# Pooled attention followed by a bilinear MoE: the planner's cost table is set to other values

## The chip, the cores and the metric

The kernel runs on one core of a Trainium2 chip. The metric is the device time in microseconds (us) of one execution; a figure is the median of several timed runs. A profile is one further execution, taken by the hardware profiler. Engines: PE is TensorE, with PEld its weight loads; DVE is VectorE, ACT is ScalarE, POOL is GpSimd, and SP is SyncE, which here only issues DMAs.

## The reference

Attention over 4 batches, 8 heads, 1152 positions and head width 64, with queries averaged in pairs (576 per head), feeds a bilinear layer of 1536 hidden columns; all in float32:

```python
q_pool = q.reshape(B, H, S // 2, 2, D).mean(axis=3)
scores = (1 / sqrt(D)) * q_pool @ k.transpose(0, 1, 3, 2)
attn = softmax(scores)                     # with + 1e-9 below the fraction
x = (attn @ v) as (4 * 576, 512)           # tokens x model width
out = ((x @ w_a) * (x @ w_b)) @ w_out      # 512 -> 1536 -> 512
```

## The kernel before

**Work.** A head pair p (16 of them, four per batch) is one step of attention. Its 576 queries and two heads are nine softmax blocks of 128 rows by 1152 keys, 144 in all. For a block, TensorE makes the scores (`qk`, `qk_rest`, L535 in float32 for batch 0 and L538 in f16 pieces for the other batches) into a PSUM tile `sps` that holds two blocks. VectorE scales them into SBUF with the row's minimum of the negated score (`sm_max`, L566), ScalarE takes the exponential with its row sum (`sm_exp`, L573), VectorE makes the reciprocal (`sm_sum`, `sm_rec`, L577 and L583), ScalarE writes the f16 high part of the probability (`sm_hi`, L586) and VectorE the low part (`sm_lo`, L590). SP then issues a transposing DMA of both parts (`transpose`, L596). When the blocks of a span of 256 or 320 queries are transposed, TensorE multiplies them with V (`pv`, 19 products, L622 and L632) into the one PSUM tile `xps`, ScalarE copies half of it out (`x_copy`, L641) and VectorE adds the other half (`x_add`, L647). ScalarE and GpSimd split x into f16 parts, and VectorE rescales them (`x_scale`, L684).

**MoE.** Nine token tiles of 256 tokens: two per batch (even and odd), and tile 8 with the 64 left over of each batch. A tile needs x of all four pairs of its batch. It is 24 steps of 12 products (`moe_mm`, L722), each pair of them gated by ScalarE and VectorE (`moe_a` L729, `moe_g` L734), and then 12 output steps of 6 products (`moe_o`, L748) on parts that ScalarE and GpSimd make (L739, L742). The f16 or rounded parts of the weights are made once, in the time of the first passes (`prep_w`, L423 to L495).

**Order.** Nothing of this order is written by hand. Every step is a task of a planner: `add(engine, duration, key, function, ..., r=, w=)` records what it reads and writes. `Plan.order` simulates five in-order engines, always giving an engine the ready task with the lowest key. It uses the durations, the table `LAT` for the delay from the end of a task on one engine (row) to the start of one that needs it on another (column), and for SP's tasks `DMA_START`, the issue time `gen`, one shared DMA channel that a transfer holds for its duration, `DMA_END` and a task's own `lag`. A task with `port=True` on VectorE keeps GpSimd's port tasks away while it runs. From each forward run the keys are made anew by a run backward in time; 20 trials with noise on the keys follow, 3 sweeps each, and the order of the shortest simulated run is emitted. Each engine then executes its own tasks strictly in that order, and waits where an input is late. The lines in question:

```python
start, length = self.run(key, False)
if best is None or length < best[0]:
    best = (length, key, start)
```

Of the kernel before, what the change touches and what calls it, by code (L numbers as in the profile page):

```python
# [19 lines left out]
NQ = S // 2  # L20
# [167 lines left out]
def kernel(  # L188
# [143 lines left out]
    def prep_qk(ps_, key):  # L332
        n = ps_.q1 - ps_.q0
        if ps_.split:
            u = f"ksc{ps_.u}"
            add("SP", 2.5, key - 3, load_k, (ps_.p, 0), w=["kn0"])
            add("SP", 2.5 * n / NQ, key - 3, load_q, (ps_.p, ps_.q0, ps_.q1), w=["qraw"])
            add("POOL", 0.1 + 1.55 * n / NQ, key, q_sum, (0, n), r=["qraw"], w=["qs0"])
            add("DVE", 1.35, key, k_max, (), r=["kn0"], w=["kmx0"])
            add("DVE", 0.1 + 0.6 * n / NQ, key, q_max, (n,), r=["qs0"], w=["kmx1"])  # L340
            add("PE", 0.45, key - 2, k_sum, (), r=["kmx0", "kmx1", "ones"], w=["xps"])
            add("DVE", 0.7, key - 2, k_scale, (ps_.u,), r=["xps"], w=[u])
            return
        if not ps_.again:
            add("SP", 2.5, key - 3, load_k, (ps_.p, ps_.jk), w=[f"kn{ps_.jk}"])
        add("SP", 2.5 * n / NQ, key - 3, load_q, (ps_.p, ps_.q0, ps_.q1), w=["qraw"])
        add("POOL", 0.1 + 1.55 * n / NQ, key, q_sum, (ps_.jq, n), r=["qraw"], w=[f"qs{ps_.jq}"])

    def split_qk(ps_, key):
        n = ps_.q1 - ps_.q0  # L350
        if ps_.split:
            u = f"ksc{ps_.u}"
            add("ACT", 1.25, key, k_hi, (ps_.u,), r=["kn0", u], w=["kn1"])
            add("ACT", 0.1 + 0.55 * n / NQ, key, q_hi, (ps_.u, n), r=["qs0", u], w=["qs1"])
            add("DVE", 1.45, key, k_lo, (ps_.u,), r=["kn0", u, "kn1"], w=["kn1l"], port=True)
            add("DVE", 0.1 + 0.65 * n / NQ, key, q_lo, (ps_.u, n), r=["qs0", u, "qs1"], w=["qs1l"], port=True)
# [43 lines left out]
    def prep_vmax(p, new, key):  # L400
        add("SP", 2.5, key - 3, load_v, (p,), w=["vraw"])
        if new:
            add("DVE", 1.3, key, v_max, (p,), r=["vraw"], w=[f"vmx{p}"])
            add("PE", 0.45, key - 2, v_sum, (p,), r=[f"vmx{p}", "ones"], w=["xps"])
            add("DVE", 0.5, key - 2, v_scale, (p,), r=["xps"], w=[f"vsc{p}"])
            if p % NP == NP - 1:
                b = p // NP
                add("DVE", 0.5, key, v_batch, (b,), r=[f"vsc{NP * b + j}" for j in range(NP)], w=[f"vb{b}"])

    def prep_v(p, key):  # L410
        add("ACT", 1.25, key, v_hi, (p,), r=["vraw", f"vsc{p}"], w=["vsh"])
        add("DVE", 1.4, key, v_lo, (p,), r=["vraw", "vsh", f"vsc{p}"], w=["vsl"], port=True)
# [85 lines left out]
    def prep_w(f, key):  # L498
        for m in range(3):
            n = 3 * f + m  # L500
            z, rw = f"z{zi(n)}", f"raw{n % NRAW}"
            add("SP", 2.2, key - 4, w_load, (f, m, n), w=[rw])
            add("ACT", 0.66, key, w_abs, (n,), r=[rw], w=[z])
            if m < 2:
                add("DVE", 0.74, key, w_max, (f, m, n), w=[z, f"wmx{f}{m}"])
            add("ACT", 0.66, key, w_tail, (n,), w=[rw + "l"], r=[rw])
            add("POOL", 2.45, key, w_sign, (n,), w=[rw + "l"], r=[rw], port=False)
            add("DVE", 0.68, key, w_join, (n,), r=[rw, rw + "l"], w=[z], port=True)
            if m == 1:
                add("DVE", 0.2, key, w_mag, (f,), r=[f"wmx{f}0", f"wmx{f}1"], w=[f"wal{f}"])  # L510
                add("PE", 0.45, key - 5, w_sum, (f,), r=[f"wal{f}", "ones"], w=["xps"])
                add("DVE", 0.2, key - 5, w_scale, (f,), r=["xps"], w=[f"wsd{f}"])
                add("DVE", 0.17, key, w_inv, (f,), r=[f"wsd{f}"], w=[f"wsc{f}"])
        for m in range(3):
# [4 lines left out]
            add("ACT", 0.7 if m < 2 else 0.66, key, w_hi, (f, m, n), r=[z] + ws, w=[f"w{f}{m}h"] + last)  # L519
            if m < 2:  # L520
                add("DVE", 0.73, key, w_lo, (f, m, n), r=[z, f"w{f}{m}h"] + ws, w=[f"w{f}{m}l"] + last, port=True)
            else:
                add("POOL", 1.6, key, w_lo, (f, m, n), r=[z, f"w{f}{m}h"], w=[f"w{f}{m}l"])
# [127 lines left out]
    def unit(ps_, e, c0, runs, key):  # L651
# [4 lines left out]
        add("PE", 0.155 + 2.16 * w / 384, key - 9, pv, (e, c0, w),  # L656
# [29 lines left out]
    def x_scales(b, which, key):  # L686
        for c in range(NP):
            for m in which:
                t = {"even": 0, "odd": 1, "rest": 2}[m]
                x = f"x{b % 2}{c}{t}" if t < 2 else f"xr{b}{c}"  # L690
                add("DVE", 0.35 if t < 2 else 0.15, key, x_scale, (NP * b + c, t), r=[f"vb{b}"], w=[x + "h", x + "l"], port=True)

    def x_split(ps_, which, key):
# [8 lines left out]
        add("ACT", 0.1 * len(which) + 0.6 * n, key, x_hi, (p, j, which), r=xs, w=[x + "h" for x in names] + alias)  # L702
        add("POOL", 0.1 * len(which) + 1.4 * n, key, x_lo, (p, j, which), r=xs + [x + "h" for x in names],
# [66 lines left out]
    def moe_ab(t, f0=0, f1=NF):  # L770
        bs = [t // 2] if t < 8 else list(range(B))
        xs = [f"x{t // 2 % 2}{c}{t % 2}{hl}" if t < 8 else f"xr{b}{c}{hl}" for b in bs for c in range(KC) for hl in "hl"]
        for f in range(f0, f1):
# [7 lines left out]
            for m in range(2):  # L781
                add("PE", 1.308, key + m, moe_mm, (t, f, m, j), r=r, w=[f"acc{j}"])
            add("ACT", 0.42 if t < 8 else 1.1, -1000, moe_a, (t, f, j), r=[f"acc{j}"] + scs, w=[f"g{f}"] + ([f"raw{1 + f // 4}"] if t == 0 and f >= 4 else []))
            add("DVE", 0.42 if t < 8 else 1.0, -1000, moe_g, (t, f, j), r=[f"acc{j}"] + scs, w=[f"g{f}"])

    def moe_last(t):
        key = 1000 + 3 * len(steps)
        for f in range(NF):
            j = len(outs) % NG
            outs.append((t, f))  # L790
            add("ACT", 0.41, key - 20, moe_gh, (f, j), r=[f"g{f}"], w=[f"gh{j}"])
            add("POOL", 0.72, key - 20, moe_gl, (f, j), r=[f"g{f}", f"gh{j}"], w=[f"gl{j}"])
            add("PE", 1.39, key - 1, moe_o, (f, j, f == 0, f == NF - 1),
# [159 lines left out]
```

## Time and profile before

| what | value |
|---|---|
| timed runs, median of 3 | 935.23 us (935.16 to 935.75) |
| profiled execution, its own time | 939.15 us |
| its span, first to last instruction | 937.4 us |
| PE, DVE, ACT, POOL busy | 792.7, 710.0, 600.6, 265.0 us |
| mean granted TensorE clock | 0.922 of full speed |

Busy time is the union of an engine's records; idle time has a releaser, the instruction or DMA that ended the wait. In-order queues mean that an instruction which waits holds up all behind it on its engine, whether they could run or not.

### The profile page before, as it was taken

How to read it: one execution, taken by the hardware profiler on the slowest of the kernel's cores; microseconds unless marked ns; L12 is line 12 of the kernel's file. 1: busy time of each engine (PE TensorE's matmuls, PEld its weight loads, DVE VectorE, ACT ScalarE, POOL GpSimd, SP SyncE). 2: the span in 40 equal slices, each digit the busy share in tenths (PEclk: the TensorE clock that was granted, in tenths of full speed). 3: DMA queues.
4: the chain of work that ended last, by engine and by line, in shares of the span. 5: the costliest groups of instructions: out<-in, count | busy, mean ns of one | idle time of the engine just before them, and what ended most of it. 6: DMA issues, size and time to landing. Idle time of an engine off the chain costs nothing.

```text
span 937.4 us, 15587 instructions
## 1 busy us (share of the span) xinstructions
PE 792.7 (85%) x5856; PEld 562.4 (60%) x5856; DVE 710.0 (76%) x1352; ACT 600.6 (64%) x973; POOL 265.0 (28%) x228
## 2 busy tenths in 40 slices
PE   4546436998789988669999999899999998999997
PEld 2323224665456755337766776576677666877885
DVE  6699999996799889998999799989889873112010
ACT  5677977966577768857787687667867762232212
POOL 4547687622311012111023113201310231110303
PEclk9666667999789999969999999999999999999999
DMA  7999799886989889987878979979786674000100
GB/s 254 235 205 243 201 236 221 222 188 121 198 174 157 155 164 195 206 167 146 174 156 167 176 152 161 199 130 175 150 162 141 103 151 76 1 23 2 23 1 23
DMA packets 353644, 141.40 MB, mean 151 GB/s; under 512 B 338208, under 2 KB 340256, under 8 KB 353568
## 3 DMA queue, kind: packets, MB, share of 16 engines
q1 hardware_dynamic: 353568, 140.40, 71.5%
q8 instruction: 46, 0.75, 0.3%
q14 instruction: 30, 0.25, 0.1%
HBM read 50.72 MB, written 4.72 MB: 59 GB/s over the span
## 4 chain that ended last, share of the span: by engine, by line
PE 50%; DVE 8%; issue 3%; DMA 2%; ACT 2%; POOL 0%; ACTq 0%; DVEq 0%
PE ab L722 24%; PE ab L748 12%; PE sps L538 7%; PE xps L622 4%; DVE p L590 2%; PE xps L632 2%; DVE s L566 2%; DMA pt<-p 2%; ACT p L586 1%; ACT g L729 0%; DVE k L315 0%; DVE x L647 0%; DVE g L734 0%; DVE o L754 0%; ACT s L573 0%
## 5 line engine op out<-in xcount | busy, mean ns | idle before, releaser
L722 PEld LDWEIGHTS <-wab 128*128 128x128 f16 x2592 | 248.9, 98 | 42.6 <-issue 6.2
L722 PE MATMUL ab<-xt,wab 128*128 128x256 f16 x2304 | 267.0, 274 | 2.8 <-DVE o L754 1.6
L590 DVE SCALAR_TENSOR_TENSOR p<-s,st,p 128x1152 f16<-128x1152 f32 x144 | 212.8, 1484 | 9.9 <-ACT p L586 9.6
L573 ACT ACTIVATE s<-s,st 128x1152 f32<-128x1152 f32 x144 | 179.9, 1250 | 56.3 <-DVE s L566 55.4
L586 ACT ACTIVATE p<-s,st 128x1152 f16<-128x1152 f32 x144 | 178.2, 1245 | 22.1 <-DMA pt<-p 7.8
L742 POOL TENSOR_TENSOR gl<-g,gh 128x256 fp32r<-128x256 f32 x108 | 95.9, 892 | 308.6 <-ACT gh L739 299.2
L566 DVE TENSOR_SCALAR_CACHE_REDUCE s<-sps,ksc 128x1152 f32<-128x1152 f32 x108 | 152.8, 1414 | 20.6 <-PE sps L538 18.5
L748 PE MATMUL ab<-wo,gh 128*128 128x512 f32 x432 | 144.4, 416 | 4.9 <-DVE g L734 4.9
L538 PE MATMUL sps<-k,q 64*128 64x512 f16 (+3 forms) x1080 | 122.0, 339 | 29.9 <-DVE s L566 25.1
L729 ACT ACTIVATE g<-ab,cc 128x256 f32<-128x256 f32 (+1 forms) x144 | 56.0, 417 | 106.0 <-PE ab L722 105.7
L622 PE MATMUL xps<-pt,vs 128*128 128x256 f16 (+1 forms) x576 | 91.4, 310 | 37.0 <-DMA pt<-p 17.2
L538 PEld LDWEIGHTS <-q 64*128 64x128 f16 (+1 forms) x1080 | 58.6, 99 | 102.9 <-issue 63.2
L734 DVE SCALAR_TENSOR_TENSOR g<-ab,cc,g 128x256 f32<-128x256 f32 (+1 forms) x144 | 56.2, 412 | 75.3 <-ACT g L729 74.7
L535 PE MATMUL sps<-k,q 64*128 64x512 f32 (+3 forms) x240 | 71.4, 675 | 41.5 <-DVE s L566 33.4
L622 PEld LDWEIGHTS <-vs 128*128 128x128 f16 x576 | 58.3, 106 | 59.9 <-issue 39.4
L748 PEld LDWEIGHTS ab<-wo,gh 128*128 128x128 f32 x432 | 78.0, 192 | 26.5 <-DVE g L734 2.6
L748 PE MATMUL ab<-wo,gl 128*128 128x512 f32 x216 | 86.7, 402 | 0.0
L535 PEld LDWEIGHTS sps<-k,q 64*128 64x128 f32 (+1 forms) x240 | 33.2, 236 | 79.1 <-DVE s L566 37.0
L739 ACT ACTIVATE gh<-g 128x256 fp32r<-128x256 f32 x108 | 43.9, 411 | 52.0 <-PE ab L748 50.9
L286 POOL TENSOR_TENSOR q<-qraw 128x576 f32<-128x576 f32 (+2 forms) x20 | 30.6, 1532 | 134.6 <-DVE q L323 42.0
L641 ACT ACTIVATE x<-xps 64x256 f32<-64x256 f32 (+2 forms) x80 | 28.1, 351 | 59.6 <-PE xps L632 54.9
L566 DVE TENSOR_SCALAR_CACHE_REDUCE s<-sps 128x1152 f32<-128x1152 f32 x36 | 48.7, 1353 | 9.1 <-PE sps L535 8.6
(88 smaller groups left out, 812.1 us busy)
## 6 DMA issues: line engine op xcount, KB each, us to landing
vraw<-in_v_dram SPq DMA_DIRECT2D x19, 576.0 KB, 4.5
k<-in_k_dram SPq DMA_DIRECT2D x19, 576.0 KB, 4.7
qraw<-in_q_dram SPq DMA_DIRECT2D x12, 576.0 KB, 5.0
g<-in_w_ab_dram SPq DMA_DIRECT2D x12, 512.0 KB, 4.5
xt<-in_w_ab_dram SPq DMA_DIRECT2D x12, 512.0 KB, 4.5
out_dram<-o SPq DMA_DIRECT2D x16, 256.0 KB, 2.8
g<-in_w_out_dram SPq DMA_DIRECT2D x6, 512.0 KB, 4.8
xt<-in_w_out_dram SPq DMA_DIRECT2D x6, 512.0 KB, 4.3
```

The costliest lines, as they stand in the source:

```text
L535: nc.tensor.matmul(out, qs[jq][rows, queries], kn[jk][rows, keys], start=True, stop=True)
L538: nc.tensor.matmul(out, qf[rows, hq - 1, queries], kf[rows, hk - 1, keys], start=(hq, hk) == (1, 1), stop=(hq, hk) == (2, 1),)
L566: nc.vector.tensor_scalar(out=s_t[sbuf(i)], in0=sps[:, at:at + S], scalar1=-1.0 / 16.0 if u is None else ksc[:, u, 4:5], scalar2=None, op0 ...
L573: nc.scalar.activation(out=s, in_=s, func=AF.Exp, scale=-1.0, bias=t[:, 0:1], accum_out=t[:, 1:2])
L586: nc.scalar.activation(out=p_t[pbuf(i)][:, 0], in_=s_t[sbuf(i)], func=AF.Copy, scale=st_t[i % NST][:, 3:4])
L590: nc.vector.scalar_tensor_tensor(out=p[:, 1], in0=s, scalar=st_t[i % NST][:, 3:4], in1=p[:, 0], op0=ALU.mult, op1=ALU.subtract)
L622: nc.tensor.matmul(xps[:, 0:w], vs[:, c, e].rearrange("p a d -> p (a d)"), pt[:, 0, c, c0:c0 + w], start=(c == 0), stop=False,)
L722: nc.tensor.matmul(dst if t < 8 else dst.rearrange("p (b n) -> p b n", b=B), wab[:, f, 1 - m, a, c], moe_x(t, b, c), start=(n == 0), stop= ...
L729: nc.scalar.activation(out=g_t[:, f, c], in_=ab[j][:, 1, c], func=AF.Copy, scale=cc[:, b, f, 0:1])
L734: nc.vector.scalar_tensor_tensor(out=g, in0=ab[j][:, 0, c], scalar=cc[:, b, f, 1:2], in1=g, op0=ALU.mult, op1=ALU.mult)
L742: nc.gpsimd.tensor_tensor(out=gl_t[j], in0=g_t[:, f], in1=gh_t[j].bitcast(F32), op=ALU.subtract)
L748: nc.tensor.matmul(acc[u], g[:, us], wo[:, f, a], start=(first and n == 0), stop=(last and n == 2))
```

## The change

It replaces the numbers of the planner's model and nothing else: the table of delays, the DMA constants, and the duration of nearly every task. Loads from HBM get an extra `lag` of 0.8 after the channel is free again. No task is added or removed. The core of the diff:

```diff
 LAT = (
-    (0.02, 0.29, 0.29, 0.29, 0.29),
-    (0.3, 0.13, 0.14, 0.17, 0.17),
...
+    (0.0, 0.22, 0.13, 0.3, 0.3),
+    (0.14, 0.115, 0.12, 0.2, 0.2),
...
-DMA_START, DMA_END = 0.72, 0.97
+DMA_START, DMA_END, LOAD_LAG = 0.72, 0.63, 0.8
...
-        add("ACT", 1.44, i - 3, sm_exp, (i,), r=[t + "m"], w=[s, t + "s"])
-        add("DVE", 0.14, i - 5, sm_sum, (i,), r=[t + "s"], w=[t + "t"])
-        add("DVE", 0.16, i - 5, sm_rec, (i,), r=[t + "t"], w=[t + "r"])
...
+        add("ACT", 1.245, i - 3, sm_exp, (i,), r=[t + "m"], w=[s, t + "s"])
+        add("DVE", 0.065, i - 5, sm_sum, (i,), r=[t + "s"], w=[t + "t"])
+        add("DVE", 0.075, i - 5, sm_rec, (i,), r=[t + "t"], w=[t + "r"])
...
-        add("SP", 2.75, i, transpose, (i,), r=[p + "h", p + "l"], w=[f"pt{slot}"], gen=0.62, block=1.02)
+        add("SP", 2.97, i, transpose, (i,), r=[p + "h", p + "l"], w=[f"pt{slot}"], gen=0.42, block=1.02)
```

Other entries, before and after: `sm_max` 1.43 to 1.34 (1.285 in batch 0), `sm_lo` 1.4 to 1.37 (1.4 in batch 0), `sm_hi` 1.245 to 1.15, `qk` 1.55 to 1.62 (1.93 to 2.0 in batch 0), `pv` of 320 queries 1.955 to 2.06, `moe_mm` 1.308 to 1.311, `moe_o` 1.39 to 1.41, loads of 576 KB 2.5 to 2.05, the output copies and the small sums on PE 0.45 to 0.2. The noise of the search is drawn from the same seed.

What this does to the order shows at three places. The first is the start of TensorE's queue: L535 are the score products of the first pass, L363 the sum that sets the scale of V. Before:

```order
L363 MATMUL xps<-vmx,one 128x2
L535 MATMUL sps<-k_69,q_73 128x512 x4
L535 MATMUL sps<-k_69,q_73 128x128 x2
L535 MATMUL sps<-k_69,q_73 128x512 x4
L535 MATMUL sps<-k_69,q_73 128x128
```

and now:

```order
L535 MATMUL sps<-k_69,q_73 128x512 x4
L535 MATMUL sps<-k_69,q_73 128x128
L363 MATMUL xps<-vmx,one 128x2
L535 MATMUL sps<-k_69,q_73 128x128
L535 MATMUL sps<-k_69,q_73 128x512 x4
```

The first score product moved ahead of V's sum; on SP, the loads of Q and K moved ahead of V's. The second place is VectorE in the first round, from the low part of the third block (p_83) to the first add of an attention product into x (L647). L566 is `sm_max`, L590 `sm_lo`, L429 and L447 weight preparation. Before:

```order
L590 SCALAR_TENSOR_TENSOR p_83<-s_77,st,p_83 128x1152
L590 SCALAR_TENSOR_TENSOR p_81<-s_75,st,p_81 128x1152
L566 TENSOR_SCALAR s_76,st<-sps 128x1152
L429 TENSOR_SCALAR wab,wmx<-wab 128x512
L455 TENSOR_SCALAR wal<-wmx 128x2
L447 SCALAR_TENSOR_TENSOR wab<-wab,xt_64 128x512
L577 TENSOR_SCALAR st<-st 128x1
L583 RECIPROCAL st<-st 128x1
L647 SCALAR_TENSOR_TENSOR x_66<-xps,x_66 64x256
```

and now the last twelve rows up to that add; the low part of the third block stands nine rows above the first of these:

```order
L447 SCALAR_TENSOR_TENSOR wab<-wab,xt_64 128x512
L429 TENSOR_SCALAR o_90,wmx<-o_90 128x512
L577 TENSOR_SCALAR st<-st 128x1
L455 TENSOR_SCALAR wal<-wmx 128x2 x2
L583 RECIPROCAL st<-st 128x1
L577 TENSOR_SCALAR st<-st 128x1
L447 SCALAR_TENSOR_TENSOR o_90<-o_90,xt_64 128x512
L583 RECIPROCAL st<-st 128x1
L429 TENSOR_SCALAR z_91,wmx<-z_91 128x512
L447 SCALAR_TENSOR_TENSOR z_91<-z_91,g 128x512
L590 SCALAR_TENSOR_TENSOR p_82<-s_76,st,p_82 128x1152
L647 SCALAR_TENSOR_TENSOR x_66<-xps,x_66 64x256
```

The add moved behind a second weight maximum and join (o_90), those of z_91, and the low part of the fifth block (p_82); above these rows, the `sm_max` of the sixth block (s_77) moved ahead of it as well. The third place is VectorE at the end of attention: p_82 and p_83 are the low parts of the last two blocks, L734 the gates of token tile 6, the L566 the last block's `sm_max`, the last L647 the adds of the last two attention products. Before:

```order
L590 SCALAR_TENSOR_TENSOR p_82<-s_76,st,p_82 128x1152
L734 SCALAR_TENSOR_TENSOR g<-ab_102,cc,g 128x256
L590 SCALAR_TENSOR_TENSOR p_83<-s_77,st,p_83 128x1152
L734 SCALAR_TENSOR_TENSOR g<-ab_101,cc,g 128x256
L647 SCALAR_TENSOR_TENSOR x_66<-xps,x_66 64x64
L647 SCALAR_TENSOR_TENSOR x_66<-xps,x_66 64x256
L734 SCALAR_TENSOR_TENSOR g<-ab_102,cc,g 128x256
L734 SCALAR_TENSOR_TENSOR g<-ab_101,cc,g 128x256
L647 SCALAR_TENSOR_TENSOR x_66<-xps,x_66 64x320
```

and now:

```order
L590 SCALAR_TENSOR_TENSOR p_82<-s_76,st,p_82 128x1152
L566 TENSOR_SCALAR s_77,st<-sps,ksc 128x1152
L577 TENSOR_SCALAR st<-st 128x1
L583 RECIPROCAL st<-st 128x1
L734 SCALAR_TENSOR_TENSOR g<-ab_102,cc,g 128x256
L734 SCALAR_TENSOR_TENSOR g<-ab_101,cc,g 128x256
L590 SCALAR_TENSOR_TENSOR p_83<-s_77,st,p_83 128x1152
L647 SCALAR_TENSOR_TENSOR x_66<-xps,x_66 64x64
L647 SCALAR_TENSOR_TENSOR x_66<-xps,x_66 64x256
```

The low part of the last block but one (p_82) moved ahead of the last `sm_max` and of the first gates of tile 6, and the last add (64x320) moved behind all twelve gates of that tile; on TensorE the last attention product stands behind all 24 product steps of tile 6, where before 14 of them stood behind it.

## Rows read from the trace of the kernel before

**Rows 1.** The page: the span, and each engine's busy time.
```profile
span 937.4 us, 15587 instructions
PE 792.7 (85%) x5856; PEld 562.4 (60%) x5856; DVE 710.0 (76%) x1352; ACT 600.6 (64%) x973; POOL 265.0 (28%) x228
```

**Rows 2.** Sums by stretch: length, busy PE, PEld, DVE, ACT, POOL, clock, DMA, GB/s.
```profile
0.00:157.70 157.70, 81.96 (x334) 44.53 (x334) 136.86 (x274) 117.16 (x175) 97.72 (x55) 0.71 0.89 227
...
424.20:791.80 367.60, 352.91 (x2905) 254.53 (x2904) 313.40 (x577) 259.13 (x405) 73.86 (x80) 0.99 0.80 153
791.80:937.40 145.60, 134.59 (x962) 113.99 (x960) 23.08 (x73) 36.97 (x107) 25.97 (x36) 0.98 0.04 12
```

**Rows 3.** Timeline of DVE: start, us, line, operation, count, [idle before it].
```profile
39.61 0.43 DVE L647 SCALAR_TENSOR_TENSOR x<-xps,x 64x256 f32<-64x256 f32 x1 [6.27 <-ACT x L641]
40.06 1.36 DVE L566 TENSOR_SCALAR_CACHE_REDUCE s<-sps 128x1152 f32<-128x1152 f32 x1
...
41.35 0.68 DVE L429 TENSOR_SCALAR_CACHE_REDUCE z<-z 128x512 f32<-128x512 f32 x1
...
44.38 0.14 DVE L577 TENSOR_SCALAR st<-st 128x1 f32<-128x1 f32 x1
```

**Rows 4.** Line L590 on DVE: count, duration in ns (min/median/max), starts.
```profile
L590 DVE SCALAR_TENSOR_TENSOR p<-s,st,p x144: 1394/1411/2559, 18.6 to 776.5; 128x1152 f16<-128x1152 f32 x144
```

**Rows 5.** Timeline of SP's queue at the start.
```profile
0.72 0.39 SPq L275 DMA_DIRECT2D vraw<-in_v_dram  x1
1.17 0.69 SPq L281 DMA_DIRECT2D qraw<-in_q_dram  x1
1.91 0.59 SPq L278 DMA_DIRECT2D k<-in_k_dram  x1
```

**Rows 6.** Timeline of PE, the first score and attention products.
```profile
7.94 4.18 PE L535 MATMUL sps<-k,q 64*128 64x512 f32 x10 [1.37 <-DMA k<-in_k_dram]
...
35.95 2.08 PE L622 MATMUL xps<-pt,vs 128*128 128x256 f16 x9 [7.98 <-DMA pt<-p]
```

**Rows 7.** Timeline of DVE near the end of batch 0.
```profile
226.02 0.23 DVE L647 SCALAR_TENSOR_TENSOR x<-xps,x 64x64 f32<-64x64 f32 x1 [3.11 <-ACT x L641]
```

**Rows 8.** Timeline of PE ahead of the first block of batch 3.
```profile
589.94 2.36 PE L538 MATMUL sps<-k,q 64*128 64x512 f16 x15 [4.14 <-DVE s L566]
...
594.81 0.73 PE L748 MATMUL ab<-wo,gh 128*128 128x512 f32 x2
...
596.41 0.34 PE L538 MATMUL sps<-k,q 64*128 64x128 f16 x3
```

**Rows 9.** Timeline of PE at the end of attention.
```profile
768.86 8.03 PE L722 MATMUL ab<-xt,wab 128*128 128x256 f16 x72
780.85 1.67 PE L622 MATMUL xps<-pt,vs 128*128 128x320 f16 x9 [3.96 <-DMA pt<-p]
...
783.80 6.09 PE L722 MATMUL ab<-xt,wab 128*128 128x256 f16 x48
789.72 1.39 PE L622 MATMUL xps<-pt,vs 128*128 128x320 f16 x9
...
791.77 4.43 PE L722 MATMUL ab<-xt,wab 128*128 128x256 f16 x39
```

**Rows 10.** Timeline of DVE at the same place.
```profile
769.33 1.41 DVE L566 TENSOR_SCALAR_CACHE_REDUCE s<-sps,ksc 128x1152 f32<-128x1152 f32 x1
...
773.51 0.48 DVE L734 SCALAR_TENSOR_TENSOR g<-ab,cc,g 128x256 f32<-128x256 f32 x1 [1.00 <-ACT g L729]
774.65 1.42 DVE L590 SCALAR_TENSOR_TENSOR p<-s,st,p 128x1152 f16<-128x1152 f32 x1 [0.66 <-ACT p L586]
```

**Rows 11.** Groups of instructions: busy us, mean ns; idle before, releaser.
```profile
L590 DVE SCALAR_TENSOR_TENSOR p<-s,st,p 128x1152 f16<-128x1152 f32 x144 | 212.8, 1484 | 9.9 <-ACT p L586 9.6
```

**Rows 12.** PE's waits: line <- releaser, us in total, times, longest.
```profile
PE sps L535 <- DVE s L566: 33.4, 18, 6.8
PE sps L538 <- DVE s L566: 25.1, 17, 4.1
```

More of the change, by code (lines that the diff above doesn't have):

```diff
@@ L352, in split_qk @@
             u = f"ksc{ps_.u}"
[L353 to L356, printed above, removed]
+            add("ACT", 1.146, key, k_hi, (ps_.u,), r=["kn0", u], w=["kn1"])
+            add("ACT", 0.075 + 0.59 * n / NQ, key, q_hi, (ps_.u, n), r=["qs0", u], w=["qs1"])
+            add("DVE", 1.33, key, k_lo, (ps_.u,), r=["kn0", u, "kn1"], w=["kn1l"], port=True)
+            add("DVE", 0.08 + 0.65 * n / NQ, key, q_lo, (ps_.u, n), r=["qs0", u, "qs1"], w=["qs1l"], port=True)
     def v_max(p):
@@ L410, in prep_v @@
     def prep_v(p, key):
-        add("ACT", 1.25, key, v_hi, (p,), r=["vraw", f"vsc{p}"], w=["vsh"])
-        add("DVE", 1.4, key, v_lo, (p,), r=["vraw", "vsh", f"vsc{p}"], w=["vsl"], port=True)
+        add("ACT", 1.146, key, v_hi, (p,), r=["vraw", f"vsc{p}"], w=["vsh"])
+        add("DVE", 1.36, key, v_lo, (p,), r=["vraw", "vsh", f"vsc{p}"], w=["vsl"], port=True)
     def w_load(f, m, n):
@@ L518, in prep_w @@
             last = [f"z{NZ + m}"] if f == NF - 1 and m < 2 else []
[L519 removed]
+            add("ACT", 0.615 if m < 2 else 0.525, key, w_hi, (f, m, n), r=[z] + ws, w=[f"w{f}{m}h"] + last)
             if m < 2:
[L521 removed]
+                add("DVE", 0.7, key, w_lo, (f, m, n), r=[z, f"w{f}{m}h"] + ws, w=[f"w{f}{m}l"] + last, port=True)
             else:
[L523 removed]
+                add("POOL", 1.3, key, w_lo, (f, m, n), r=[z, f"w{f}{m}h"], w=[f"w{f}{m}l"])
     def sbuf(i):
@@ L690, in x_scales @@
                 x = f"x{b % 2}{c}{t}" if t < 2 else f"xr{b}{c}"
-                add("DVE", 0.35 if t < 2 else 0.15, key, x_scale, (NP * b + c, t), r=[f"vb{b}"], w=[x + "h", x + "l"], port=True)
+                add("DVE", 0.26 if t < 2 else 0.155, key, x_scale, (NP * b + c, t), r=[f"vb{b}"], w=[x + "h", x + "l"], port=True)
     def x_split(ps_, which, key):
@@ L701, in x_split @@
         names = [name[m] for m in which]
-        add("ACT", 0.1 * len(which) + 0.6 * n, key, x_hi, (p, j, which), r=xs, w=[x + "h" for x in names] + alias)
-        add("POOL", 0.1 * len(which) + 1.4 * n, key, x_lo, (p, j, which), r=xs + [x + "h" for x in names],
+        add("ACT", 0.06 * len(which) + 0.55 * n, key, x_hi, (p, j, which), r=xs, w=[x + "h" for x in names] + alias)
+        add("POOL", 0.2 * len(which) + 0.9 * n, key, x_lo, (p, j, which), r=xs + [x + "h" for x in names],
             w=[x + "l" for x in names] + alias)
```

78 lines of the change are left out of this document (39 added, 39 removed).

## Prediction

> **What bounds the kernel now.** I read the page first, then the sums by stretch, then who waits for whom, then the timeline at the longest waits. TensorE is busy 792.7 us of 937.4 and VectorE 710.0 [rows 1], and neither is the limit all the way. The stretches [rows 2] show it. Up to 157.7 us no MoE product can run, since the first token tile needs all four head pairs of batch 0: VectorE is busy 136.86 of 157.70 us, TensorE 81.96, at a mean granted clock of 0.71 of 2.4 GHz, a mixture of its two levels. From 424.2 to 791.8 TensorE is busy 352.91 of 367.60 at 0.99 with VectorE at 313.40. After 791.8 VectorE has 23 us of work left and TensorE runs the last three token tiles alone. So the time is a VectorE-paced start, a TensorE-paced middle and a TensorE-only end, and a new order can win only what these engines idle at such places: 20.8 us on VectorE in the first stretch, 14.7 us on TensorE in the third. The end of 145.6 us holds nothing for the planner except what it starts with.
>
> The change touches no instruction, only numbers with which the planner lays out five in-order queues. So I ask whether the new numbers are nearer to the chip, and what the new order does where the old one idles.
>
> **Are the numbers nearer?** An instruction's record ends when its result is written; the next one on the engine may start before that. sm_max (L566) has a record of 1.36 us at 40.06 and the next instruction starts at 41.35 [rows 3], so it holds the engine for 1.29 us; the old table says 1.43, the new 1.285 (1.34 where the scores come from f16 pieces). sm_lo (L590) has a median record of 1.411 us [rows 4], the old table has 1.4, the new 1.37 and 1.4. Per softmax block the VectorE entries add up to 1.43 + 0.14 + 0.16 + 1.4 = 3.13 before and 1.34 + 0.065 + 0.075 + 1.37 = 2.85 now, over 144 blocks 40 us less. Of 710 us that is 6% by which the old planner took VectorE for busier than it is, and by so much it misplaced what other engines give to VectorE or take from it. The new one leaves less slack behind every VectorE step, which counts against it (first rival).
>
> **Part 1, the first loads.** SP issued V at 0.72, Q at 1.17 and K at 1.91 us [rows 5]; the first score product waited for K and started at 7.94 [rows 6]. Now Q and K are first, and V's issue of 0.45 us (1.17 - 0.72) stands behind them. The product stands ahead of V's little sum on TensorE, so nothing of V delays it. Gain 0.45 us; nothing is lost, since V's pieces are first needed by the product at 35.95.
>
> **Part 2, the first attention product.** The first L622 sat on TensorE for 7.98 us until a transpose landed, at 35.95 [rows 6]. The copy and the add behind it (L641, L647) stand in ScalarE's and VectorE's queues, so VectorE idled 6.27 us at 39.61 with work behind the waiting add: from 40.06 to 44.38 it ran sm_max, a weight maximum, a sm_lo and a join that had not depended on it, 4.3 us [rows 3]. In the new order all four stand ahead of that add, with a second maximum and join of 0.6 to 0.7 us each (the record at 41.35 is 0.68) [rows 3], about 5.6 us, and the second score product of that round stands ahead of the attention product on TensorE, so sm_max has its input. The cover is 5.6 of 6.27; V's scale steps, which also come ahead, bring it to about 6. I take 6.0. Bounds: 0, if the transpose lands as much later, and 6.3.
>
> **Part 3, end of batch 0.** VectorE waits 3.11 us for another such copy at 226.02 [rows 7]. In the new order two more MoE products and a score product stand between. I take half, 1.5 (0 to 3.1): this stretch is short of both engines in turn.
>
> **Part 4, score products before batch 3.** At 589.94 TensorE waits 4.14 us for VectorE; an attention product and an output product, the latter from 594.81 to 596.41, are queued behind the waiting one [rows 8]. The new order puts both ahead. The attention product needs the copy of the one before it, which VectorE made at the same late point, so I count only the output product as cover, 1.6 us (0 to 4.1).
>
> **Part 5, the last softmax blocks.** At 780.85 TensorE waits 3.96 us for a transpose, after six steps of token tile 6 [rows 9]. On VectorE the sm_lo that feeds it starts at 774.65, behind the last block's sm_max at 769.33 and a gate (L734) that waited 1.00 us [rows 10]. In the new order it stands ahead of both: 1.34 + 1.00 + 0.48 = 2.8 us earlier. The last attention product moves behind all of tile 6, where it can't wait. I take 2.8 (0 to 4.9: the wait and 0.9 us by which this product, 2.95 us from 780.85 to 783.80, was slower than the next one of its kind, 2.05 from 789.72 to 791.77).
>
> **The sum.** 0.45 + 6.0 + 1.5 + 1.6 + 2.8 = 12.35 us. Against it stands what a tighter order brings anew. I price it at two collisions of VectorE with GpSimd of the largest kind seen, 2 x (2.559 - 1.411) = 2.3 us [rows 4]. 10.05 us remain. The profiled execution took 939.15 us, 1.75 of it outside its span, and would come to about 929; the timed runs have a median of 935.23, 3.9 us below it, so I forecast 925.0. By the bounds alone the listed places are worth 0 to 18.9 us (0.45 + 6.3 + 3.1 + 4.1 + 4.9).
>
> **A rule that speaks against it.** L590's records run from 1.394 to 2.559 us [rows 4]: some take nearly a microsecond more than their fellows, and their mean of 1.484 [rows 11] against the median of 1.411 is 10.5 us over 144. The Trainium skill (SBUF — State Buffer, Who interferes with whom) says that a VectorE instruction with two SBUF inputs and a GpSimd instruction that reads SBUF exclude each other, the later one waiting for the whole of the other. By it, a planner that believes 1.37 us and lets the weights' GpSimd pass (port=False) run beside anything, as before and after, gains nothing in early VectorE work; by the rows those 10.5 us are in both orders. The rival below holds what happens if they grow.
>
> **Rivals.**
> *Slack lost, slower.* The queues are in order, and a long entry leaves room for late inputs. TensorE already waits 33.4 + 25.1 us for sm_max [rows 12]. If each of the 144 blocks now meets its score product too early by the 0.09 us cut from its entry (1.43 to 1.34), that is 13 us more on the engine that sets the middle and end; less the 6.5 us of parts 1 and 2 it gives 935.2 + 13 - 6.5 = 942. It decides once the sum of those two waits exceeds 58.5 + 13. For it: parts 2 and 5 are themselves such waits. Against: the cut entries are what the rows show, so the input is in truth not late. Chance 0.13.
> *Collisions doubled, slower.* 10.5 us more on VectorE in the early stretches, less 6.5: 939. Chance 0.05.
> *The waits only move.* Five places are repaired and as many others open, since four in five of TensorE's tasks stand at another place of its queue: 935, chance 0.08.
> *The whole order gets better.* Beyond the five places, VectorE's 20.8 us before the first MoE step and TensorE's 14.7 us in the third stretch [rows 2] both shrink by two thirds: 24 us, 911. For it: all engines' entries changed in the same direction. Against: part of this idle time is latency that no order removes, such as the wait for the first loads. Chance 0.20.
>
> **How the numbers follow.** Forecast 925.0, chance 0.54, its own range 917 to 932. Faster by over 0.2% (1.9 us, about what a measurement of this kernel tells from none): 0.54 + 0.20 = 0.74. Within: 0.08. Slower: 0.13 + 0.05 = 0.18. A range of 910 to 940 leaves out half of the first rival and a little of the fast case.
>
> **What would show it.** Part 1: first score product near 7.5 us. Part 2: no VectorE wait over 2 us at the first L647, the first MoE product before 155. Part 4: TensorE idle under 8 us in the stretch that was 424.2 to 791.8. Part 5: no wait over 2 us for the last transposes, and only two token tiles and an output pass on TensorE behind the last attention product (by the new table 48 x 1.311 + 36 x 1.41 = 114 us). Wrong if the first MoE product comes no earlier than 157 us, or if TensorE's waits for sm_max exceed 70 us. Records of L590 with a mean over 1.55 us would mean collisions.

## The result and the profile after

The changed kernel takes 910.9 us (median of 4 runs, 907.2 to 912.3) where the kernel before took 935.2 us beside it (930.9 to 935.8): ratio 0.974, 95% interval 0.970 to 0.979. The forecast was 925.0 us. The sign was right, and the gain of 24 us was more than twice the 10 expected. The number is that of the fourth rival (911 us: "the whole order gets better"), but not for its reason, and the gain did not come out of the five places of the sum.

The page of the changed kernel, against [rows 1]: the span is 27.2 us shorter, while the busy times of the engines hardly move.

```profile
span 910.2 us, 15571 instructions
PE 785.7 (86%) x5856; PEld 558.6 (61%) x5856; DVE 705.4 (77%) x1352; ACT 597.6 (66%) x973; POOL 265.2 (29%) x228
```

VectorE has lost 4.6 us of busy time and TensorE 7.0; on either engine the rest of the 27.2 was idle time. To see where, I cut both traces at the same pieces of work: the end of softmax block 53's `sm_lo` (the end of batch 1; 54 of 144 blocks done), and that of block 143, the last. The sums by stretch are, in columns: length, busy PE, PEld, DVE, ACT, POOL, clock, DMA share, GB/s. Before:

```profile
0.00:337.50 337.50, 240.39 (x1537) 154.25 (x1538) 293.72 (x556) 242.33 (x369) 151.13 (x94) 0.83 0.88 202
337.50:777.90 440.40, 406.75 (x3275) 286.27 (x3275) 391.22 (x720) 319.74 (x495) 87.34 (x98) 0.97 0.83 160
777.90:937.40 159.50, 145.53 (x1046) 121.85 (x1045) 25.09 (x78) 38.51 (x111) 26.58 (x37) 0.97 0.07 17
```

and after:

```profile
0.00:314.40 314.40, 226.80 (x1480) 144.16 (x1482) 287.49 (x555) 240.83 (x368) 146.85 (x93) 0.84 0.94 215
314.40:759.50 445.10, 413.76 (x3314) 291.99 (x3311) 392.27 (x721) 317.76 (x495) 91.93 (x99) 0.97 0.83 161
759.50:910.20 150.70, 145.15 (x1068) 122.49 (x1066) 25.63 (x79) 38.98 (x112) 26.45 (x37) 0.99 0.06 15
```

The first stretch is 23.1 us shorter, the middle 4.7 longer, the end 8.8 shorter. VectorE is the busier engine of the first stretch: it did the same work (556 and 555 instructions) with 26.9 us idle instead of 43.8, and 6.2 us less busy. In the middle TensorE is the bound: it has 39 records and 7.0 us more to do there, because the shorter first stretch let fewer matmuls run beside it (1480 for 1537). In the end TensorE's idle time falls from 14.0 us (159.50 - 145.53) to 5.6 (150.70 - 145.15).

VectorE's waits in the first stretch (line <- releaser: us in total, times, longest), before:

```profile
DVE x L647 <- ACT x L641: 10.9, 5, 6.3
DVE s L566 <- PE sps L535: 8.6, 8, 2.3
DVE vmx L359 <- DMA vraw<-in_v_dram: 5.4, 2, 3.7
DVE s L566 <- PE sps L538: 4.6, 4, 1.5
...
L590 DVE SCALAR_TENSOR_TENSOR p<-s,st,p 128x1152 f16<-128x1152 f32 x54 | 83.8, 1557 | 2.4 <-ACT p L586 2.2
```

and after:

```profile
DVE vmx L359 <- DMA vraw<-in_v_dram: 8.1, 2, 7.1
DVE x L647 <- ACT x L641: 3.9, 3, 3.0
DVE z L429 <- ACT z L423: 2.4, 1, 2.4
DVE s L566 <- PE sps L535: 1.9, 4, 0.9
DVE s L566 <- PE sps L538: 1.2, 2, 0.8
...
L590 DVE SCALAR_TENSOR_TENSOR p<-s,st,p 128x1152 f16<-128x1152 f32 x54 | 78.2, 1454 | 1.0 <-ACT p L586 0.9
```

Three things went. The waits of `sm_max` (L566) for score products fell from 13.2 us in 12 waits to 3.1 in 6: -10.1. The waits of the add (L647) fell by 7.0. And the `sm_lo` (L590, the last row: 54 of them, busy us, mean ns) lost 5.6 us of stretched records. Against them V's first load costs 2.7 us more and one weight maximum (L429) 2.4.

Part of this is the one run that was profiled. It took 939.15 us, 3.9 over the median of its kernel, and three experiments below that keep the old order up to block 53 reach that point at 332.1 to 332.8 us, not 337.5. Against these three the first stretch gains 18.3 us (332.4 to 314.1, with the two runs of the new order that follow), of which 4.9 is busy time and 13.4 idle: -7.8 by `sm_max`, -7.0 by the add.

In the end only one releaser is left on TensorE (waits from block 143's end, line <- releaser). Before:

```profile
PE xps L622 <- DMA pt<-p: 4.0, 1, 4.0
PE ab L748 <- DVE g L734: 3.5, 3, 2.0
PE ab L722 <- DVE o L754: 1.6, 2, 0.8
PE ab L722 <- DVE g L734: 0.6, 1, 0.6
```

and after:

```profile
PE ab L748 <- DVE g L734: 1.8, 2, 1.4
```

Two entries in the timeline of TensorE explain the second to fourth row of before. Token tile 8's 24 product steps (L722) begin at 828.52 and its output steps (L748) at 862.91:

```profile
828.52 5.40 PE L722 MATMUL ab<-xr,wab 128*128 128x256 f16 x48 [0.78 <-DVE o L754]
834.53 1.70 PE L722 MATMUL ab<-xr,wab 128*128 128x256 f16 x14 [0.61 <-DVE g L734]
...
862.91 0.70 PE L748 MATMUL ab<-wo,gh 128*128 128x512 f32 x2 [2.01 <-DVE g L734]
```

After, the same places at 807.37 and 838.73 have no wait:

```profile
807.37 4.85 PE L722 MATMUL ab<-xr,wab 128*128 128x256 f16 x43
...
838.73 0.70 PE L748 MATMUL ab<-wo,gh 128*128 128x512 f32 x2
```

Two accumulators take turns, and a step waits until the gate (L734) or the output copy (L754) has read the one that it wants. The old order took tile 8's hidden blocks as 1, 0, 3, 2, ..., 11, 10, the halves of the first two interleaved: it began with the accumulator that the output pass before it had used last, and ended with block 10 on accumulator 0, which the first output step wants too. The new order takes them as 0, 1, ..., 11, so that every step up to the first output step finds its accumulator free; only the second output step waits (1.37 us). From the first product step to the first output step it is 31.36 us instead of 34.39.

The busy time of the end holds one thing more. Behind the wait of 2.01 us the output pass of tile 8 ran at a mean granted clock of 0.91 and took 18.57 us. The kernel "new, then old" of the experiments below has the old order here, waits 2.00 us at the same place, and ran the pass at 1.00 in 17.04 us:

```profile
862.91:881.48 18.57, 18.57 (x72) 14.64 (x73) 0.00 (x0) 4.79 (x11) 7.40 (x10) 0.91 0.00 1
...
844.83:861.87 17.04, 17.04 (x72) 13.51 (x73) 0.00 (x0) 4.79 (x11) 7.39 (x10) 1.00 0.01 1
```

So 1.5 us of the end's gain lies in the clock of one execution, and the same wait does not always bring it.

### The profile page after: what moved, and what is told of

The parts are those of the page before. It is cut to its first block, busy times and chain, and to the rows that moved or that the text cites. A ratio compares the mean times of both kernels' runs of the same rounds, so it can differ in the third digit from the quotient of the medians.

```text
span 910.2 us, 15571 instructions
## 1 busy us (share of the span) xinstructions
PE 785.7 (86%) x5856; PEld 558.6 (61%) x5856; DVE 705.4 (77%) x1352; ACT 597.6 (66%) x973; POOL 265.2 (29%) x228
## 4 chain that ended last, share of the span: by engine, by line
PE 53%; DVE 16%; DMA 9%; issue 4%; ACT 3%; POOL 1%; SPq 0%; DVEq 0%; ACTq 0%; POOLq 0%
PE ab L722 26%; PE ab L748 10%; DMA pt<-p 8%; PE sps L538 7%; PE xps L622 6%; DVE s L566 5%; DVE p L590 5%; PE xps L632 3%; DVE k L315 1%; ACT p L586 1%; PE sps L535 1%; ACT s L573 1%; DVE q L323 1%; DVE x L647 1%; DVE g L734 1%
## 5 line engine op out<-in xcount | busy, mean ns | idle before, releaser
L722 PEld LDWEIGHTS <-wab 128*128 128x128 f16 x2592 | 249.6, 99 | 40.2 <-issue 4.0
L722 PE MATMUL ab<-xt,wab 128*128 128x256 f16 x2304 | 267.2, 274 | 1.5 <-DVE g L734 0.6
L590 DVE SCALAR_TENSOR_TENSOR p<-s,st,p 128x1152 f16<-128x1152 f32 x144 | 208.0, 1452 | 11.4 <-ACT p L586 11.2
L566 DVE TENSOR_SCALAR_CACHE_REDUCE s<-sps,ksc 128x1152 f32<-128x1152 f32 x108 | 152.6, 1413 | 11.1 <-PE sps L538 9.8
L748 PE MATMUL ab<-wo,gh 128*128 128x512 f32 x432 | 141.4, 409 | 2.5 <-DVE g L734 1.8
L538 PE MATMUL sps<-k,q 64*128 64x512 f16 (+3 forms) x1080 | 118.9, 330 | 21.3 <-DVE s L566 15.8
L622 PE MATMUL xps<-pt,vs 128*128 128x256 f16 (+1 forms) x576 | 90.2, 307 | 37.4 <-DMA pt<-p 17.6
L734 DVE SCALAR_TENSOR_TENSOR g<-ab,cc,g 128x256 f32<-128x256 f32 (+1 forms) x144 | 56.1, 413 | 74.7 <-ACT g L729 74.1
L538 PEld LDWEIGHTS <-q 64*128 64x128 f16 (+1 forms) x1080 | 56.7, 98 | 91.2 <-issue 44.8
L535 PE MATMUL sps<-k,q 64*128 64x512 f32 (+3 forms) x240 | 72.8, 683 | 45.9 <-DVE s L566 27.5
L748 PEld LDWEIGHTS ab<-wo,gh 128*128 128x128 f32 x432 | 77.2, 188 | 23.0 <-issue 2.9
L748 PE MATMUL ab<-wo,gl 128*128 128x512 f32 x216 | 86.1, 398 | 0.1
L535 PEld LDWEIGHTS sps<-k,q 64*128 64x128 f32 (+1 forms) x240 | 33.7, 236 | 83.5 <-issue 40.9
L739 ACT ACTIVATE gh<-g 128x256 fp32r<-128x256 f32 x108 | 43.3, 410 | 45.2 <-PE ab L748 42.7
L632 PE MATMUL xps<-pt,vs 128*64 128x256 f16 (+3 forms) x640 | 53.4, 303 | 0.0
```

The source lines that it names most:

```text
L535: nc.tensor.matmul(out, qs[jq][rows, queries], kn[jk][rows, keys], start=True, stop=True)
L538: nc.tensor.matmul(out, qf[rows, hq - 1, queries], kf[rows, hk - 1, keys], start=(hq, hk) == (1, 1), stop=(hq, hk) == (2, 1),)
L566: nc.vector.tensor_scalar(out=s_t[sbuf(i)], in0=sps[:, at:at + S], scalar1=-1.0 / 16.0 if u is None else ksc[:, u, 4:5], scalar2=None, op0 ...
L590: nc.vector.scalar_tensor_tensor(out=p[:, 1], in0=s, scalar=st_t[i % NST][:, 3:4], in1=p[:, 0], op0=ALU.mult, op1=ALU.subtract)
L622: nc.tensor.matmul(xps[:, 0:w], vs[:, c, e].rearrange("p a d -> p (a d)"), pt[:, 0, c, c0:c0 + w], start=(c == 0), stop=False,)
L632: nc.tensor.matmul(xps[half(u), a:b], vs[:, c, e, 0], pt[:, 1, c, c0 + a:c0 + b], start=False, stop=(c == NCH - 1),)
```

## The experiments

Two theories stood against each other. *Numbers*: the new table is nearer to the chip, so any order drawn with it is better. *Draw*: an order by this search is one draw, another seed moves the time as much as the table does, and 24 us is luck. A third question was where in the order the gain is made.

**Other seeds of the search, with either table.** The search adds noise to its keys from one seed.

```diff
-SEED, TRIALS, SWEEPS = 3, ...
+SEED, TRIALS, SWEEPS = 4, ...   # or 5
```

Old table, seed 4: 

> Old numbers, seed of the planner's noise 4 in place of 3; nothing else. Theory 'true numbers' (the 24 us come from numbers that tell the planner which order is short, whatever the noise): any seed with the old numbers stays near the kernel before, 918 to 945, and over every seed of the new numbers. Rival 'luck of the draw' (twenty noisy trials reshuffle four in five tasks, and seed 3 happened to fall well with the new numbers): seeds spread by as much as the change itself, so with the old numbers one of seeds 4 and 5 comes to 915 or less. Of eight seeds this is the one whose order looks shortest when it is laid out again with the new numbers, so it is the rival's best case: if the new numbers are also a good judge of foreign orders, 915 to 925.

Old table, seed 5: 

> Old numbers, seed 5. By 'true numbers' 930 to 950: of eight seeds its order looks longest when laid out again with the new numbers. By 'luck of the draw' anything from 905 to 945.

New table, seed 4: 

> New numbers, seed 4. By 'true numbers' 908 to 925: the new numbers rate this as the longest of eight seeds, some per cent behind seed 3, but still below the kernel before by 10 us or more. By 'luck of the draw' it falls back to 925 to 940.

New table, seed 5: 

> New numbers, seed 5, which the new numbers rate as the shortest of eight. By 'true numbers' 902 to 915, level with the changed kernel (910.9) or some us faster. By 'luck of the draw' 905 to 940, and no better than seed 4 but by chance.

Measured, in us, with the ratio to the kernel before on the same chip: old table 920.1 (0.987 [0.982, 0.992]) and 941.5 (1.010 [1.007, 1.014]); new table 923.7 (0.991 [0.988, 0.994]) and 902.5 (0.968 [0.965, 0.971]). With seed 3 the old table gives 920, 935, 942 and the new one 903, 911, 924: means of 932 and 912. Both theories hold in part. The table moves the mean of three draws by 20 us, and a draw moves the time by about 10 either way: the best old draw beats the worst new one by 3.5 us. One pair of kernels alone could not have told this. By the bounds set beforehand *Draw* failed three times (neither old seed came to 915 or less, the new seed 4 did not fall back to 925 or more, and the new seed 5 came below 905), and *Numbers* once (not every old draw lies above every new one).

But seeds 4 and 5 were not drawn blindly. As the expectations say, they are for either table the two ends of eight seeds by the new table's rating, that is, by the length of the order laid out with the new numbers. So 10 us either way is nearer to the spread of the ends than of an ordinary draw. And the rating called the order right on both sides: 4, 3, 5 with the old table, 5, 3, 4 with the new one. Each planner's own estimate (`self.estimate` in the kernel, worked out off the chip) runs the same way: 940, 957 and 963 us for the old table's 920, 935 and 942; 890, 896 and 907 for the new one's 903, 911 and 924. How well a draw fell is thus in part known to the planner, which speaks for *Numbers*; three seeds on a side do not prove it.

**Where the order makes it.** Four kernels issue a fixed list of tasks. The first takes the new order until block 53's `sm_lo` and the remaining tasks in the old order; the second the other way round; the third is old until block 143's `sm_lo` and then new. The fourth is the old order with one thing changed: the product steps of token tiles 8 and 7, and their gates, stand in their natural order.

```diff
-        for i in self.order():
+        for i in HYBRID:    # a list written out
```

New, then old: 

> The new order up to the low part of block 53 (the last block of the first half of batch 1), then all other tasks in the order of the kernel before. Theory 'early': the gain is made where VectorE paces, in batch 0 and the first half of batch 1, where block 53 was done 23.0 us sooner (337.5 to 314.4 us), and the rest only keeps it. Then 912 to 918: the tail's 7 us are missing. Rival 'late or everywhere': each stretch owes its gain to an order that fits the whole, and the joint costs what was won: 920 to 935.

Old, then new: 

> The order of before up to the low part of block 53, then all other tasks in the new order. By 'early' 925 to 931: only the tail's 7.2 us (from the last low part to the end 154.8 us before, 147.6 after) can be won. By 'late or everywhere' 915 to 922.

Old, and new for the end alone: 

> The order of before up to the low part of the last block 143, then the rest in the new order: tile 6 to the end alone is changed. If the last 150 us hold a gain of their own, apart from where they start: 5 to 7 us faster, 926 to 930. If they are only moved, as the prediction said beyond the last attention products: 2 to 3 us, 930 to 933.

Tiles 8 and 7 in natural order: 

> The order of before; only in token tiles 8 and 7 the product steps and their gates stand in their natural order (hidden block 0, 1, 2 ...; both halves of a block one after the other), as nearly so in the changed kernel. Theory 'order of the steps': in before these tiles begin with hidden block 1, whose PSUM tile is freed last (waits 0.78 and 0.61 us), mix the halves of two blocks, and end with block 10, on whose PSUM tile the first output product waits 2.0 us; the 24 steps of tile 8 took 34.39 us against 31.36 after, those of tile 7 32.68 against 31.36. So 3 to 5 us faster, 929 to 931, which is most of what the new tail alone gave (6.4). Rival 'last attention products': the new tail's gain came from tile 6 and the last transposes; then less than 1 us.

Measured: 918.6 (0.984 [0.981, 0.987]); 929.9 (0.996 [0.993, 0.998]); 927.4 (0.994 [0.991, 0.996]); 926.4 (0.993 [0.990, 0.995]); the kernel before 933.7, and 933.5 beside the fourth. The first lies 0.6 us above the 912 to 918 that "early" had asked for, the other two within what their theories asked. So the first stretch is worth 15.1 us, the end 6.4, together 21.5 of 24, and the middle of the new order nothing that shows: with it added to the end the gain is 3.9, not 6.4, and the two intervals overlap. The waits of VectorE in the first stretch repeat. With the old order until block 53 (the third kernel; its lines are shifted by 85, so L651 is `sm_max`, L732 the add, L675 `sm_lo`):

```profile
DVE x L732 <- ACT x L726: 10.6, 5, 6.1
DVE s L651 <- PE sps L620: 6.3, 5, 2.1
...
DVE s L651 <- PE sps L623: 2.1, 2, 1.3
L675 DVE SCALAR_TENSOR_TENSOR p<-s,st,p 128x1152 f16<-128x1152 f32 x54 | 82.7, 1537 | 2.7 <-ACT p L671 2.4
```

With the new order until there (the first kernel):

```profile
DVE x L732 <- ACT x L726: 2.9, 2, 2.6
...
DVE s L651 <- PE sps L620: 1.3, 4, 0.6
...
DVE s L651 <- PE sps L623: 0.4, 2, 0.2
L675 DVE SCALAR_TENSOR_TENSOR p<-s,st,p 128x1152 f16<-128x1152 f32 x54 | 78.1, 1451 | 1.2 <-ACT p L671 1.2
```

The fourth kernel shows that the order of the steps makes the end's gain: an edit of two tiles' order, with the old table and the old order everywhere else, gains 7.2 us (interval 5.1 to 9.0), more than the 3 to 5 expected. It sets the blocks in order and also ends the interleaving of the halves, so which of the two does it is not told apart. In its trace tile 8 runs as in the changed kernel, without a wait inside it (L807 are the product steps, L833 the output steps):

```profile
821.81 10.43 PE L807 MATMUL ab<-xr,wab 128*128 128x256 f16 x94
...
851.42 0.70 PE L833 MATMUL ab<-wo,gh 128*128 128x512 f32 x2
```

Its waits of TensorE after block 143:

```profile
PE xps L707 <- DMA pt<-p: 4.0, 1, 4.0
PE ab L833 <- DVE g L819: 2.1, 3, 1.4
```

The wait for the last transposes (L707 is the attention product) is as long as before, and the waits inside tile 8 are gone. Between their first product step and their first output step, tiles 8 and 7 take 31.4 us each where they took 34.4 and 32.7: 4.4 us. No step of the trace shows the rest of the 7.2.

**Which numbers make it.** Each kernel is the changed one with one group of entries set back to the old values (or the reverse), as here:

```diff
-        add("ACT", 1.245, i - 3, sm_exp, ...
+        add("ACT", 1.44, i - 3, sm_exp, ...
```

VectorE's durations old: 

> The new numbers, but VectorE's durations as before (longer, 3.13 instead of 2.85 us a block). Theory 'true numbers': VectorE paces the first 400 us, so its numbers matter most, and the planner again lays out for a VectorE that is too slow: 925 to 945. Rival 'slack': longer entries on VectorE leave room for late inputs, so this keeps the gain or adds to it: 900 to 912.

The old table with VectorE's durations new: 

> The old numbers with VectorE's durations alone set to the new values. If VectorE's numbers make the gain by themselves: 908 to 922. If the numbers work only together (delays, ScalarE and DMA too): 924 to 938.

New table, VectorE's durations 1.1 times as long: 

> The new numbers with every VectorE duration 1.1 times as long (about the sum that the old table had), so that the proportions within VectorE stay. Theory 'true numbers': VectorE against the other engines decides what is laid beside what, so most of the gain goes: 920 to 940. Rival 'proportions within VectorE': 905 to 916. Rival 'slack': 905 or less.

Delays between engines old: 

> The new numbers, but the five rows of delays between engines as before (LAT). If every group is needed: 925 to 938. If VectorE's entries carry the gain: 903 to 918. The old delays are longer by 0.07 to 0.17 us from TensorE and VectorE to VectorE and ScalarE, so the planner again takes chains for longer than they are; but that changes every chain alike, so I lean to a loss of a third: 915 to 925.

ScalarE's durations old: 

> The new numbers, but ScalarE's durations as before (1.44 + 1.245 a block instead of 1.245 + 1.15, and both output copies). If every group is needed: 925 to 938. If VectorE's carry it: 903 to 918. ScalarE is never the limit, so a third of the loss at most: 912 to 922.

DMA durations and constants old: 

> The new numbers, but the DMA constants and transfer times as before. If every group is needed: 925 to 938. If VectorE's carry it: 903 to 918. TensorE's waits for transposes are 17.2 us before and 17.6 after, so the DMA's numbers changed little that can be seen: 905 to 918.

TensorE's and GpSimd's durations old: 

> The new numbers, but TensorE's and GpSimd's durations as before; these changed least (some 5% on scores and attention products, 0.45 to 0.2 on the small sums). If every group is needed: 925 to 938. If VectorE's carry it: 903 to 918, where I expect it.

| kernel | us | ratio to before | end of block 53, us |
|---|---|---|---|
| VectorE old | 936.3 | 1.002 [1.000, 1.005] | 330.0 |
| only VectorE new | 937.5 | 1.004 [1.002, 1.005] | 322.8 |
| VectorE x 1.1 | 940.4 | 1.007 [1.005, 1.009] | 315.8 |
| delays old | 933.8 | 1.000 [0.997, 1.003] | 327.0 |
| ScalarE old | 929.6 | 0.996 [0.993, 0.999] | 324.1 |
| DMA old | 926.7 | 0.994 [0.991, 0.997] | 330.1 |
| TensorE, GpSimd old | 922.5 | 0.988 [0.985, 0.992] | 317.7 |

No group carries the gain alone. VectorE's new entries by themselves give nothing; taking them, the delays, ScalarE's or the DMA's back loses 16 to 25 us, two thirds or all of the gain. For the last four kernels I had leaned to smaller losses than were measured, in every case. TensorE's and GpSimd's cost 11.6, but 922.5 lies within what another seed gives with the whole new table (902 to 924), so their part is not settled; and each of the seven is one draw. What is consistent is the direction: seven of seven are slower than the changed kernel. With the DMA entries old, TensorE's first score product starts at 9.14 us instead of 5.58, and its waits for K's loads are 10.6 us, of which 9.1 are this first one, counted from the start:

```profile
PE sps L535 <- DMA k<-in_k_dram: 10.6, 2, 9.1
```

With VectorE's durations 1.1 times as long block 53 still ends at 315.8, but TensorE then waits 28.0 us for transposes where the changed kernel waits 17.6, and the last `sm_lo` ends 40 us into token tile 6 (808.3, from 768.0) instead of 9 (759.5, from 750.7):

```profile
PE xps L622 <- DMA pt<-p: 28.0, 11, 6.4
```

**A wider search.** With the new table and 60 trials from seed 25: 

> The new numbers, 60 trials and seed 25, which they rate as the shortest of 120 seeds. Theory 'true numbers': their rating holds on the chip, so this is at or below seed 5 (902.5): 893 to 904. Rival 'luck of the draw' (rating says nothing below some per cent): somewhere in the range of seeds 3 to 5, 902 to 924, most likely 912.

Measured: 903.4 (0.967 [0.964, 0.970]), the same as seed 5's 902.5. Both are about 8 us below the changed kernel (0.968 and 0.967 against 0.974; the first one's interval touches the changed kernel's); seed 25 is the best-rated of 120, seed 5 of eight, so a search fifteen times as wide won nothing that the chip shows.

## Why the prediction was right and wrong

**The view of the stretches** was right as far as it went: a VectorE-paced start, a TensorE-paced middle, a TensorE-only end, in which an order wins only what the pacing engine idles [rows 2]. The steps that failed came with it and behind it. It passed over the time from 157.7 to 424.2 us, for which the sum had nothing but part 3's 1.5. Most of the gain was made there. From the first MoE product to the end of block 53, before and after:

```profile
157.70:337.50 179.80, 158.43 (x1205) 109.72 (x1204) 156.86 (x283) 125.17 (x194) 53.40 (x40) 0.94 0.86 179
...
154.08:314.40 160.32, 145.50 (x1145) 100.11 (x1146) 150.12 (x277) 123.40 (x190) 36.27 (x35) 0.99 0.91 185
```

That is 19.5 of the 23.1 us, with 60 matmuls fewer in it; VectorE's idle time fell from 22.9 to 10.2 and TensorE's from 21.4 to 14.8. The first MoE product itself hardly moved. It starts at 154.1 and 155.2 us in the two runs of the new order, and at 154.1, 155.1, 155.6 and 157.7 in the four that are old up to there (three hybrids and the kernel before). So parts 1 and 2 changed their places, and VectorE's idle time up to this product fell (from 19.2 to 20.8 us in the four, to 16.7 and 17.2), but no earlier MoE start shows; the sign "before 155" came true and tells nothing.

And where it did look, the sum priced the longest single wait of five places (0.45 + 6.0 + 1.5 + 1.6 + 2.8) and left out the many short ones on the same engine. Up to block 53 `sm_max` waited 12 times for its score product, 13.2 us, none of them over 2.3; this was in the trace, and one grouped row of VectorE's waits up to block 53 would have shown it as large as the add's 10.9. The new numbers took 8 to 10 us of it.

**"Beside the five places" against "less than the bounds".** The listed bounds were 18.9 us in all; the measured gain passed them, so no sizing of those five could have been right.

**The end.** The sentence that the end "holds nothing for the planner except what it starts with" was false, and the natural-order kernel shows by how much: 5 to 9 us by the timed runs. The group of waits of that stretch would have shown 5.7 us behind L734 and L754 besides the 4.0 of the transposes. By the steps, the changed kernel's end gains 3.0 in tile 8 (34.39 to 31.36), 1.3 in tile 7 (32.68 to 31.36), 1.5 in three output passes (54.9 to 53.4, the clock of that one execution), 1.5 in the transposes (part 5) and 1.6 behind the last product (5.4 to 3.8), together about the 8.8 us by which the time from block 143's `sm_lo` to the last instruction fell (159.5 to 150.7).

**Part by part.** Part 1 was mis-sized: 2.4 us instead of 0.45. The sum had V's issue of 0.45 us (K's came 0.43 earlier, 1.48 for 1.91) and not that K's load lands sooner with only Q ahead of it:

```profile
0.72 0.71 SPq L281 DMA_DIRECT2D qraw<-in_q_dram  x1
1.48 0.58 SPq L278 DMA_DIRECT2D k<-in_k_dram  x1
2.10 0.43 SPq L275 DMA_DIRECT2D vraw<-in_v_dram  x1
```

The first score product, against [rows 6] at 7.94:

```profile
5.58 4.17 PE L535 MATMUL sps<-k,q 64*128 64x512 f32 x10 [5.58 <-DMA k<-in_k_dram]
```

From K's issue to that product it is 4.10 us, where with V and Q ahead it was 6.03 (1.91 to 7.94). VectorE's maximum of V waits 7.09 us for its load, to 7.94, where it waited 3.72, so "nothing is lost" was wrong too; and yet the first `sm_max` stands at 9.79 where it was at 12.2.

Part 2 came as forecast in its place. The add no longer waits (0.43 us at 41.33, against 6.27 us of idle time in [rows 3]), and the product before it waited 4.33 instead of 7.98 us. But a weight maximum now waits 2.35 us ahead of it, a place that the sum did not have, so that the two together gave 3.9 and not 6.0:

```profile
38.08 0.69 DVE L429 TENSOR_SCALAR_CACHE_REDUCE z<-z 128x512 f32<-128x512 f32 x1 [2.35 <-ACT z L423]
...
41.33 0.43 DVE L647 SCALAR_TENSOR_TENSOR x<-xps,x 64x256 f32<-64x256 f32 x1
```

Part 3 failed in its place: the wait of 3.11 us [rows 7] is 2.99 us at 210.91. The add's waits together fell by 7.0 where parts 2 and 3 had 7.5, so their sum came near by luck, with both shares wrong.

Part 4's wait of 4.14 us [rows 8] is gone, but its check failed. I had asked for under 8 us of idle TensorE in the third stretch; between 400 and 770 it is still 16.8:

```profile
400.00:770.00 370.00, 353.18 (x2904) 255.33 (x2903) 312.95 (x578) 258.04 (x408) 75.59 (x80) 0.99 0.81 154
```

This agrees with the hybrid kernels, by which the new order wins nothing in the middle.

Part 5 came in half: the last transposes are waited for 2.51 us where it was 3.96 [rows 9], 1.5 us and not 2.8:

```profile
758.60 2.56 PE L622 MATMUL xps<-pt,vs 128*128 128x320 f16 x9 [2.51 <-DMA pt<-p]
```

The last attention product did move behind all of tile 6, and ends at 790.4 without a wait.

**The charge of 2.3 us for collisions** had the wrong sign. [rows 11] had a mean of 1484 ns over 144 `sm_lo`; now:

```profile
L590 DVE SCALAR_TENSOR_TENSOR p<-s,st,p 128x1152 f16<-128x1152 f32 x144 | 208.0, 1452 | 11.4 <-ACT p L586 11.2
```

The median is unchanged (1411 and 1414 ns), so the sum over the median fell from 10.5 to 5.5 us. Records over 1.5 us were 20 before and 12 after, and each of the 32 has a GpSimd instruction beside it. That fits the rule of the Trainium skill (SBUF — State Buffer, Who interferes with whom) that such instructions of the two engines exclude each other. Of the 256 shorter records 83 have one beside them too, so the overlap by itself does not tell which will be long. "Collisions doubled" falls.

**The other rivals.** *Slack lost* falls by its own test. TensorE's waits for `sm_max` were to exceed 71.5 us; they fell from 58.5 [rows 12] to 43.3:

```profile
PE sps L535 <- DVE s L566: 27.5, 15, 4.0
PE sps L538 <- DVE s L566: 15.8, 13, 3.9
```

*The waits only move* holds for the middle alone. *The whole order gets better* had the right size by luck. Neither of the two idle times that it named shrank by two thirds: VectorE's before the first MoE product went from 20.8 to 16.7 us, and TensorE's in the third stretch did not fall. The gain came between them and at the end, which it left out. In its spirit, many places and not five, it was right, and 0.20 was too small for that: I read the table as right or wrong engine by engine, while the experiments suggest that its groups work together.

**What stays open.** The first stretch and the end, tried apart, make 21.5 of 24.3 us, within the intervals. How much of the 24 is the table and how much seed 3 can't be told from three seeds on either side, two of them picked as the ends of eight: their means differ by 20, with a spread of about 10 within each. Why the new order is shorter between the first MoE product and block 53 is told by the waits that went; which of the many moved tasks does it no run shows.

## What to carry to other kernels

Before you price single places, group all waits of the engine that paces a stretch: many waits of 1 or 2 us weigh as much as the one that stands out, and a better order removes them together. Let the stretches cover the whole span, and look at each in this way, one too where a single engine seems to run by itself; there the order in which accumulators are taken and freed is worth checking first. A planner's table is best corrected in all its groups at once (durations from start to start, delays, transfers): here every group set back came out slower, in one draw each. An order that comes out of a noisy search is one draw: time several seeds with either table before you credit the table, and keep the fastest by the chip. The better table's rating can help to pick them: here it put three seeds in the right order on either side.

## What the hardware showed that I had not expected

K's first load, always 576 KB, took 4.0 us from issue to landing with Q's 256 KB ahead of it, 5.9 with V's 576 and Q's, and 7.1 with a weight load of 512 and Q's (the kernel with the DMA entries old). What stands ahead matters, though not by its bytes alone. So the order of the first loads moves the first score product by more than the issue time that it saves.

Entries of VectorE that are too long by a tenth made the program 29 us longer (940.4 against 910.9), though it has the same instructions and only their order changed: more than the whole gain of the new table, if in one draw.
